# Recurrent state by one scan per head pair, and rows placed by matmul in the first unit

## The chip, the cores and the metric

The kernel runs on one core of one Trainium2 chip. The metric is the device time of one execution in microseconds. TensorE's granted clock has two levels, 1.2 and 2.4 GHz; a granted clock of 1.00 in the profile is the higher one.

## The reference

Three layers follow each other: a recurrent attention with decay over 4 sequences of 768 tokens with 8 heads of 48, a feed-forward layer with g = h cos h, and one with the largest of three products.

```python
def _attn_ref(q, k, v, alpha) -> np.ndarray:
    ...
    for t in range(S):
        state = alpha[:, :, t, :, None] * state + np.einsum('bhd,bhe->bhde', k[:, :, t], v[:, :, t])
        y[:, :, t] = np.einsum('bhd,bhde->bhe', q[:, :, t], state)

def _moe_ref(x, w_in, w_out) -> np.ndarray:
    h = x @ w_in
    g = h * np.cos(h)
    return (g @ w_out).astype(np.float32)

def _moe2_ref(x, w1, w2, w3, w_out) -> np.ndarray:
    h = np.maximum(np.maximum(x @ w1, x @ w2), x @ w3)
    return (h @ w_out).astype(np.float32)
```

There are 3072 tokens, d_model is 384, d_ff is 2048 in the first layer and 768 in the second. All inputs are fp32.

## The kernel before

The tokens are cut into six units of 512 (eight chunks of 64; twelve chunks make a sequence). A unit goes through attention, through 16 tiles of the first layer (one per 128 columns of w_in) and later through the second layer. To keep precision a matrix is split into a high and a low fp32r part, and a product is three matmuls: high by high, high by low, low by high.

**Attention** (`att`) is called for each unit and for four head pairs, pair 3 first, then 0, 1, 2. For a pair the two heads lie on partitions 0 to 47 and 64 to 111. Scans on VectorE build g, the products of decays from a token to the end of its chunk (L370 in the first unit, L380 in the others), and their counterpart in al (L376, L385). GpSimd multiplies k and q by them (L372, L384, L387). TensorE transposes k (L392), makes the scores (L404) and each chunk's own contribution to the state (L409). ScalarE or VectorE and GpSimd mask the scores into the tile a (L416, L417, L420).

The state s at the start of each chunk is then built step by step in `state`: eight instructions on VectorE (L426, L428), each of which takes the one before it, multiplies by the chunk's whole decay g[:, c, 0] and adds the chunk's own contribution out of PSUM. The state that the values need, d, is s times g once more: on GpSimd (L440), two products of 48 x 384 per pair, and in the first unit on ScalarE for the first head, chunk by chunk (L435). TensorE adds scores by v (L453) and d by q (L459) in PSUM. ScalarE takes the high part of the result into the tile xt (L474). The low part is taken by VectorE (L481), or in the first unit by a product with minus the identity (L477) and ScalarE (L479).

A tile of xt has 128 rows for each of the pairs 0, 1 and 2: 2 x 48 of the pair itself, and in the two gaps of 16 rows the rows of pair 3. Pair 3 is therefore made first, into the tile yy, and two DMAs per pair (L488) copy its rows into the gaps. The first layer's products wait for them.

**The first layer** (`moe1`) makes for tile i nine matmuls into a bank of PSUM (L501 to L503: three pieces of x by three products), then cos by a sine of half the argument: L508 and L510, L511 on ScalarE, L509 and L513 or L517 on VectorE, the high part gh on ScalarE and the low part gl on GpSimd (L515, for the tiles below GLP1) or VectorE (L523). Nine matmuls (L528 to L530) add into three banks acc. In the first unit the weights come in while the tiles run: `weight` loads a block (SP queue, L312), unpacks it in three instructions on VectorE (L315 to L317), and splits it on ScalarE (L320) and GpSimd (L321). Each tile has two blocks, one of w_in and one of w_out; 32 blocks in all.

**The order.** Nothing of this runs in the order of the source. Each operation is put into `Program` with a modelled duration, its reads and writes, and a due time; `Program.order` lists them for all engines, and picks on each engine, among the operations that are ready by the model, the one that is due first. The constants at the top (W1E, MOE_EARLY, ATT0, ATTS, GLP1) set due times and choices. On the chip each engine runs its own list in this fixed order.

## Time and profile before

| | |
|---|---|
| median of three runs | 818.61 us (815.3 to 819.21) |
| profiled execution | 816.90 us, its span 815.2 us |
| TensorE, VectorE, ScalarE, GpSimd busy | 791.5, 476.4, 360.9, 192.8 us |
| mean granted clock of TensorE | 0.985 |

A busy matmul row is not TensorE at its peak, because matmuls are pipelined; the distance between the starts of two products tells more. The times in a timeline count from the start of the span. A wait that is put down to an instruction is put down to the one that came last. VectorE's instructions overlap a little: the next one can start before the record of the last one ends.

### The profile page before, as it was taken

To read this page: it belongs to the slowest core of one execution; us is meant where nothing else is said; L and a number is where in the kernel's file an instruction comes from. 1 tells how busy PE (TensorE), PEld (TensorE's weight loads), DVE (VectorE), ACT (ScalarE), POOL (GpSimd) and SP (SyncE) were. 2 spreads that over 40 slices of the span, in tenths; PEclk is the share of its full clock that TensorE was granted. 3 is DMA by queue.
4 is the path that set the end of the run, shared out by engine and by line. 5 is a ranking of instruction groups with operands and counts; after the bars stand their busy time and mean duration, and the time that the engine had idled before them with its cause. 6 is when DMAs were issued, how large, how long until landed. Compare 5 with 4: busy or idle time off the path is not lost.

```text
span 815.2 us, 15114 instructions
## 1 busy us (share of the span) xinstructions
PE 791.5 (97%) x6168; PEld 646.0 (79%) x6168; DVE 476.4 (58%) x924; ACT 360.9 (44%) x667; POOL 192.8 (24%) x191
## 2 busy tenths in 40 slices
PE   7679999999999999999999999999999999999998
PEld 6567778888878878888888788888888888888886
DVE  7988999765786587667679955452232222322221
ACT  4575655555645565555577746531121121112121
POOL 7777876530231023101123200110000000000000
PEclk8789999999999999999999999999999999999999
DMA  9745564430242033103135600412020020200001
GB/s 273 214 132 174 182 209 141 130 93 5 88 147 54 2 115 108 43 1 108 34 107 161 221 23 1 156 58 86 26 83 27 14 91 26 78 27 13 14 27 39
DMA packets 26661, 71.86 MB, mean 88 GB/s; under 512 B 3488, under 2 KB 3488, under 8 KB 26592
## 3 DMA queue, kind: packets, MB, share of 16 engines
q1 hardware_dynamic: 26592, 70.90, 26.9%
q8 instruction: 48, 0.79, 0.4%
q14 instruction: 21, 0.17, 0.1%
HBM read 54.37 MB, written 14.16 MB: 84 GB/s over the span
## 4 chain that ended last, share of the span: by engine, by line
PE 84%; DVE 6%; POOL 4%; issue 2%; DMA 2%; ACT 2%; SPq 0%; POOLq 0%; DVEq 0%; ACTq 0%
PE ps L580 9%; PE ps L579 9%; PE ps L581 9%; PE acc L528 7%; PE ps L501 7%; PE acc L530 7%; PE acc L529 7%; PE ps L503 7%; PE ps L502 7%; PE ps L603 3%; PE ps L602 3%; PE ps L604 3%; PE ps L459 2%; PE ps L404 1%; PE ps L453 1%
## 5 line engine op out<-in xcount | busy, mean ns | idle before, releaser
L501 PE MATMUL ps<-xt,wih 128*128 128x512 f32 x288 | 116.3, 404 | 3.7 <-ACT kt L395 2.2
L528 PE MATMUL acc<-gh,woh 128*128 128x512 f32 x288 | 116.5, 405 | 0.7 <-DVE yy L538 0.5
L530 PE MATMUL acc<-gl,woh 128*128 128x512 f32 x288 | 112.8, 392 | 0.5 <-DVE gl L523 0.4
L502 PE MATMUL ps<-xt,wih 128*128 128x512 f32 x288 | 113.2, 393 | 0.0
L503 PE MATMUL ps<-xt,wil 128*128 128x512 f32 x288 | 113.0, 392 | 0.0
L529 PE MATMUL acc<-gh,wol 128*128 128x512 f32 x288 | 112.4, 390 | 0.0
L517 DVE SCALAR_TENSOR_TENSOR ps<-q,ps 128x512 f32<-128x512 f32 x76 | 52.7, 694 | 56.9 <-ACT q L511 56.7
L589 DVE TENSOR_TENSOR ps<-t,ps 128x512 f32<-128x512 f32 x36 | 25.0, 696 | 103.6 <-PE ps L581 103.5
L510 ACT ACTIVATE q<-q 128x512 f32<-128x512 f32 x96 | 60.5, 631 | 52.3 <-DVE q L509 52.0
L508 ACT ACTIVATE q<-ps 128x512 int32<-128x512 f32 x96 | 57.1, 595 | 57.0 <-PE ps L503 54.6
L509 DVE SCALAR_TENSOR_TENSOR q<-q,ps 128x512 f32<-128x512 int32 x96 | 65.7, 685 | 21.1 <-ACT q L508 20.8
L590 ACT ACTIVATE h<-ps 128x512 fp32r<-128x512 f32 x36 | 21.5, 598 | 112.1 <-DVE ps L589 112.0
L523 DVE TENSOR_TENSOR gl<-ps,gh 128x512 fp32r<-128x512 f32 x76 | 52.1, 686 | 26.7 <-PE ps L503 15.9
L501 PEld LDWEIGHTS ps<-xt,wih 128*128 128x128 f32 x288 | 54.7, 190 | 16.4 <-ACT kt L395 3.2
L440 POOL TENSOR_TENSOR d<-s,g 48x384 f32<-48x384 f32 x44 | 37.0, 842 | 125.5 <-DVE s L428 123.7
L587 DVE TENSOR_TENSOR t<-t,ps 128x512 f32<-128x512 f32 x36 | 24.8, 688 | 71.2 <-PE ps L581 70.4
L528 PEld LDWEIGHTS acc<-gh,woh 128*128 128x128 f32 x288 | 54.0, 188 | 14.9 <-DVE yy L538 2.3
L518 ACT ACTIVATE gh<-ps 128x512 fp32r<-128x512 f32 x76 | 45.4, 598 | 44.0 <-DVE ps L517 41.5
L530 PEld LDWEIGHTS acc<-gl,woh 128*128 128x128 f32 x288 | 54.1, 188 | 13.5 <-DVE gl L523 1.4
L503 PEld LDWEIGHTS ps<-xt,wil 128*128 128x128 f32 x288 | 54.7, 190 | 11.8
L502 PEld LDWEIGHTS ps<-xt,wih 128*128 128x128 f32 x288 | 54.9, 190 | 10.4
L529 PEld LDWEIGHTS acc<-gh,wol 128*128 128x128 f32 x288 | 54.1, 188 | 9.9
(122 smaller groups left out, 1579.4 us busy)
## 6 DMA issues: line engine op xcount, KB each, us to landing
raw<-in_wt SPq DMA_DIRECT2D x56, 384.0 KB, 3.3
kq<-in_qka SPq DMA_DIRECT2D x23, 448.0 KB, 4.2
x1d<-yy SPq DMA_DIRECT2D x18, 512.0 KB, 2.6
xt<-x1d SPq DMA_DIRECT2D x18, 512.0 KB, 4.4
v<-in_vv SPq DMA_DIRECT2D x22, 256.0 KB, 3.2
al<-in_qka SPq DMA_DIRECT2D x24, 228.4 KB, 2.7
outT<-y SPq DMA_DIRECT2D x18, 256.0 KB, 2.0
xt<-yy SPq DMA_DIRECT2D x36, 64.0 KB, 2.6
```

Of the source, the lines that this page charges most:

```text
L501: pe.matmul(ps, wi["h"][:, f, cc], xt[:, cc, 0], start=(cc == 0), stop=False)
L502: pe.matmul(ps, wi["h"][:, f, cc], xt[:, cc, 1], start=False, stop=False)
L503: pe.matmul(ps, wi["l"][:, f, cc], xt[:, cc, 0], start=False, stop=(cc == NR - 1))
L508: op("Act", act(HB, True), lambda: se.activation(q.bitcast(I32), ps, AF.Copy, scale=INV2PI), [hk], [qk], m)
L509: op("DVE", dve(HB), lambda: ve.scalar_tensor_tensor(q, q.bitcast(I32), -TWOPI, ps, ALU.mult, ALU.add), [hk], [qk], m)
L510: op("Act", act(HB), lambda: se.activation(q, q, AF.Sin, scale=0.5), (), [qk], m)
L528: pe.matmul(acc[c], oh, gh, start=(f == 0), stop=False)
L529: pe.matmul(acc[c], ol, gh, start=False, stop=False)
L530: pe.matmul(acc[c], oh, gl, start=False, stop=(f == NF1 - 1))
L579: pe.matmul(ps, w2t["h"][m][:, f, cc], xt[:, cc, 0], start=(cc == 0), stop=False)
L580: pe.matmul(ps, w2t["h"][m][:, f, cc], xt[:, cc, 1], start=False, stop=False)
L581: pe.matmul(ps, w2t["l"][m][:, f, cc], xt[:, cc, 0], start=False, stop=(cc == NR - 1))
```

## The change

1. The state of a pair is made by one scan (L457 of the changed kernel). ScalarE copies the eight own contributions out of PSUM into s, which now has the layout [partition, column e, chunk], ten places per column (two copies, L455; a carry of the last state from the second unit on, L453). GpSimd spreads g[:, c, 0] over the columns into a tile gx (L442), with zeros where a sequence begins (L448). The scan runs over 480 elements: add, then multiply. What it leaves is s times g already, so d is a mere copy with the chunk outermost (L465): by ScalarE in units 0 to 5 as the constants stand.
2. In the first unit the rows of pair 3 are not copied by DMA. A tile sel (in the space of the second gl tile) is built at the start by ScalarE, and four matmuls of 256 columns per pair (L501) add the selected rows of yy into the pair's PSUM before ScalarE takes the high part. In the other units the DMAs stay.
3. There are two g tiles instead of three, one inv instead of two. The constants GLP1 (20 to 24), W1E (10 to 14), MOE_EARLY (4 to 2) and ATTS (2.5 to 3) change, and a coefficient of the modelled matmul time.

```diff
-NQ, NG, NRAW, NIN, NV, NGS = 3, 2, 3, 3, 2, 3
+NQ, NG, NRAW, NIN, NV, NGS = 3, 2, 3, 3, 2, 2
...
-GLP1 = 20
+GLP1 = 24
...
-W1E = 10
-MOE_EARLY = 4
+W1E = 14
+MOE_EARLY = 2
...
-ATTS = 2.5
+ATTS = 3
...
+    sel = gl_b[1][:, 0:(NP - 1) * P].rearrange("p (k n) -> p k n", k=NP - 1)
...
-    s_b = [ap.tile([PR, NC, D], F32, name=f"s{p}") for p in range(NP)]
+    s_b = [ap.tile([PR, D, NC + 2], F32, name=f"s{p}") for p in range(NP)]
+    x_b = [ap.tile([PR, D, NC + 2], F32, name=f"gx{i}") for i in range(1)]
...
-        for c in range(NC - 1):
-            op("DVE", 0.2, lambda c=c: state(c), [rk[c % 2], *kgs, (*sk, c)], [(*sk, c + 1)], t0 + 0.25)
...
-                op("Pool", pool(NC * D), lambda j=j, w=w: ge.tensor_tensor(d[w, j], s[w], g[w, :, 0:1].to_broadcast([D, NC, D]), ALU.mult),
...
+        def spread(e):
+            gc = g.rearrange("p c t -> p t c")[:, 0:1].to_broadcast([PR, D, NC])
...
+                ge.tensor_copy(gx[:, :, 0:NC], gc)
+            for c in range(NC):
+                if firsts[c]:
...
+                        ge.memset(gx[:, :, c:c + 1], 0.0)
...
+        if u:
+            op("Act", 0.25, lambda: se.activation(s[:, :, 0:1], s[:, :, NC:NC + 1], AF.Copy), (), [sk], t0 - 0.5)
+        for h in range(2):
+            op("Act", act(AO, True) + 0.05, lambda h=h: se.activation(
+                s[:, :, 1 + h:NC + 1:2], r[h][0:PR, 0:AO].rearrange("p (i e) -> p e i", e=D), AF.Copy), [rk[h], *([sk] if h else [])], [(sk, h) if h else sk], t0 + 0.22)
+        op("DVE", 0.07 + 0.00208 * D * (NC + 2), lambda: ve.tensor_tensor_scan(
+            s.rearrange("p e c -> p (e c)"), s.rearrange("p e c -> p (e c)"), gx.rearrange("p e c -> p (e c)"), 0.0, ALU.add, ALU.mult),
+           [xk, (sk, 1)], [sk], t0 + 0.25, port=True)
...
+                op("Act", act(NC * D), lambda j=j, w=w, x=x: se.activation(d[w, j], x, AF.Copy), [sk], [(dk, j)], t0 + 0.25)
...
+        moved = u < SELU and p < NP - 1
...
+                        pe.matmul(y[h][:, 0:HB // 2], sel[:, p], yy_b[0][:, x, HB // 2 * h:HB // 2 * (h + 1)], start=False, stop=(x == 1), skip_group_check=True)
...
-        if p < NP - 1:
+        if p < NP - 1 and not moved:
...
+                se.activation(sel[:, p], ident, AF.Copy, scale=0.0)
+                for i in range(2):
+                    row = 16 * (2 * p + i)
+                    src = UP * (row // D) + row % D
+                    se.activation(sel[:, p, UP * i + D:UP * (i + 1)], ident[:, src:src + 16], AF.Copy)
```

The order of the instructions changes on every engine. Buffer numbers in the rows below are the build's own and differ between the two kernels.

TensorE at the end of the first unit's attention, before: acc is where the last pair's values lie, minus gives their low part (L477), and the pieces of x are multiplied by the first weights (L501). The last row is the third piece of tile 0.

```order
L477 MATMUL acc_96<-xt_451,minus 128x256
L501 MATMUL ps_100<-xt_451,wih 128x512
L502 MATMUL ps_100<-xt_451,wih 128x512
L503 MATMUL ps_100<-xt_451,wil 128x512
L501 MATMUL ps_98<-xt_451,wih 128x512
L502 MATMUL ps_98<-xt_451,wih 128x512
L503 MATMUL ps_98<-xt_451,wil 128x512
L392 MATMUL ps_99<-ident,kq_112 128x112 x4
L501 MATMUL ps_99<-xt_451,wih 128x512
L502 MATMUL ps_99<-xt_451,wih 128x512
L503 MATMUL ps_99<-xt_451,wil 128x512
L501 MATMUL ps_100<-xt_451,wih 128x512
```

After: the values with d (L483), the four selecting products (L501), the low part (L510), and the scores of the next unit.

```order
L483 MATMUL acc_95<-yy_91,d_126 48x64 x2
L483 MATMUL acc_96<-yy_91,d_126 48x64 x2
L501 MATMUL acc_95<-yy_90,gl_89 128x256 x2
L501 MATMUL acc_96<-yy_90,gl_89 128x256 x2
L510 MATMUL acc_95<-xt_448,minus 128x256
L510 MATMUL acc_96<-xt_448,minus 128x256
L415 MATMUL ps_100<-kq_110 64x64
L415 MATMUL ps_102<-kq_110 64x64
```

The selecting products stand between the values and the low part, in TensorE's own list; before, TensorE's list went on to products that wait for DMAs.

VectorE in the middle of the second unit's first pair, before: state steps (s_125) between the steps of a weight block and scans.

```order
L315 TENSOR_SCALAR ps_99<-raw_93 128x384
L428 SCALAR_TENSOR_TENSOR s_125<-s_125,g_114,ps_101 112x48
L316 SCALAR_TENSOR_TENSOR ps_99<-raw_93,ps_99 128x384
L428 SCALAR_TENSOR_TENSOR s_125<-s_125,g_114,ps_102 112x48
L317 SCALAR_TENSOR_TENSOR raw_93<-raw_93,ps_99 128x384
L428 SCALAR_TENSOR_TENSOR s_125<-s_125,g_114,ps_101 112x48
L380 SCALAR_TENSOR_TENSOR g_113<-al_107,one_103 112x520
L428 SCALAR_TENSOR_TENSOR s_125<-s_125,g_114,ps_102 112x48
L383 RECIPROCAL inv_104<-g_113 112x8
```

After, at the state of the same pair (s_123): one row stands for the eight.

```order
L326 TENSOR_SCALAR ps_98<-raw_92 128x384
L327 SCALAR_TENSOR_TENSOR ps_98<-raw_92,ps_98 128x384
L546 SCALAR_TENSOR_TENSOR q_84<-q_84,ps_99 128x512
L328 SCALAR_TENSOR_TENSOR raw_92<-raw_92,ps_98 128x384
L457 SCALAR_TENSOR_TENSOR s_123<-s_123,gx_124 112x480
L326 TENSOR_SCALAR ps_102<-raw_93 128x384
L546 SCALAR_TENSOR_TENSOR q_85<-q_85,ps_101 128x512
L327 SCALAR_TENSOR_TENSOR ps_102<-raw_93,ps_102 128x384
L542 SCALAR_TENSOR_TENSOR q_83<-q_83,ps_100 128x512
L328 SCALAR_TENSOR_TENSOR raw_93<-raw_93,ps_102 128x384
```

The scan comes between two weight blocks, and the two-step chain of gelu (L546, L542) goes on around it.

TensorE at tile 13 of the first unit, before: the transposes of a pair (L392), the nine products of tile 13 (L501 to L503, ps_98), behind them the values of another pair (L453).

```order
L503 MATMUL ps_102<-xt_451,wil 128x512
L392 MATMUL ps_98<-ident,kq_110 128x112 x4
L501 MATMUL ps_98<-xt_451,wih 128x512
L502 MATMUL ps_98<-xt_451,wih 128x512
L503 MATMUL ps_98<-xt_451,wil 128x512
L501 MATMUL ps_98<-xt_451,wih 128x512
L502 MATMUL ps_98<-xt_451,wih 128x512
L503 MATMUL ps_98<-xt_451,wil 128x512
L501 MATMUL ps_98<-xt_451,wih 128x512
L502 MATMUL ps_98<-xt_451,wih 128x512
L503 MATMUL ps_98<-xt_451,wil 128x512
L453 MATMUL ps_99<-a_121,v_117 64x64 x2
```

After: the output products (acc) of one more tile come first, then tile 13 (L534 to L536, ps_100).

```order
L561 MATMUL acc_97<-gh_87,woh 128x512
L562 MATMUL acc_97<-gh_87,wol 128x512
L563 MATMUL acc_97<-gl_89,woh 128x512
L534 MATMUL ps_100<-xt_448,wih 128x512
L535 MATMUL ps_100<-xt_448,wih 128x512
L536 MATMUL ps_100<-xt_448,wil 128x512
L534 MATMUL ps_100<-xt_448,wih 128x512
L535 MATMUL ps_100<-xt_448,wih 128x512
L536 MATMUL ps_100<-xt_448,wil 128x512
```

In the list after, the values group that followed tile 13 and one more score group stand before this place too: up to tile 13's first product there are 9 groups of scores, 8 of values and 12 tiles of output products (before: 8, 7 and 11).

## Rows read from the trace of the kernel before

**Rows 1.** The page, busy tenths in 40 slices of 20.4 us, two engines

```profile
PE   7679999999999999999999999999999999999998
...
DVE  7988999765786587667679955452232222322221
```

**Rows 2.** Table of stretches: us, busy of each engine, clock, DMA share, GB/s

```profile
0.00:60.00 60.00, 44.55 (x728) 36.97 (x729) 50.89 (x121) 34.04 (x86) 46.54 (x55) 0.80 0.69 206
60.00:115.00 55.00, 51.51 (x506) 40.60 (x507) 52.19 (x115) 32.11 (x63) 44.44 (x39) 1.00 0.59 182
115.00:450.00 335.00, 335.00 (x3354) 271.64 (x3353) 248.59 (x499) 194.97 (x352) 90.54 (x88) 1.00 0.28 88
...
650.00:700.00 50.00, 50.00 (x222) 41.41 (x221) 13.06 (x19) 8.97 (x15) 0.00 (x0) 1.00 0.12 48
```

**Rows 3.** Timeline of TensorE: start, length, engine, line, operation, tiles, shapes

```profile
78.95 0.49 PE L530 MATMUL acc<-gl,woh 128*128 128x512 f32 x1 [0.15 <-POOL gl L515]
...
81.25 0.39 PE L529 MATMUL acc<-gh,wol 128*128 128x512 f32 x1
...
84.91 0.39 PE L503 MATMUL ps<-xt,wil 128*128 128x512 f32 x1
...
86.63 0.39 PE L529 MATMUL acc<-gh,wol 128*128 128x512 f32 x1
```

**Rows 4.** Timeline, end of the first attention unit (several engines)

```profile
43.46 0.51 SPq L488 DMA_DIRECT2D xt<-yy  x1
...
46.63 0.50 PE L501 MATMUL ps<-xt,wih 128*128 128x512 f32 x1 [0.69 <-ACT kt L395]
...
53.36 0.64 PE L392 MATMUL ps<-ident,kq 112*128 112x112 f32 x4 [3.04 <-DVE raw L317]
...
59.88 0.50 PE L528 MATMUL acc<-gh,woh 128*128 128x512 f32 x1
```

**Rows 5.** Timeline around the weights of tile 13

```profile
107.37 2.42 DVE L385 TENSOR_TENSOR_SCAN al<-al,inv 112x520 f32<-112x520 f32 x1
...
107.67 1.02 POOL L321 TENSOR_TENSOR wol<-raw,woh 128x384 fp32r<-128x384 f32 x1
...
110.95 0.55 DVE L317 SCALAR_TENSOR_TENSOR raw<-raw,ps 128x384 uint32<-128x384 uint32 x1
...
112.56 1.01 POOL L321 TENSOR_TENSOR wil<-raw,wih 128x384 fp32r<-128x384 f32 x1
...
113.88 0.50 PE L501 MATMUL ps<-xt,wih 128*128 128x512 f32 x1 [1.53 <-ACT kt L395]
```

**Rows 6.** Timeline of VectorE, state steps among weight steps and a scan

```profile
43.42 0.55 DVE L315 TENSOR_SCALAR ps<-raw 128x384 uint32<-128x384 uint32 x1
43.88 0.26 DVE L428 SCALAR_TENSOR_TENSOR s<-s,g,ps 112x48 f32<-112x48 f32 x1
44.05 0.55 DVE L316 SCALAR_TENSOR_TENSOR ps<-raw,ps 128x384 uint32<-128x384 uint32 x1
...
45.35 1.23 DVE L380 TENSOR_TENSOR_SCAN g<-al,one 112x520 f32<-112x520 f32 x1
```

**Rows 7.** Groups of instructions by line: busy us, mean ns, idle before them

```profile
L509 DVE SCALAR_TENSOR_TENSOR q<-q,ps 128x512 f32<-128x512 int32 x96 | 65.7, 685 | 21.1 <-ACT q L508 20.8
L440 POOL TENSOR_TENSOR d<-s,g 48x384 f32<-48x384 f32 x44 | 37.0, 842 | 125.5 <-DVE s L428 123.7
L385 DVE TENSOR_TENSOR_SCAN al<-al,inv 112x520 f32<-112x520 f32 x20 | 27.0, 1350 | 0.3
L320 ACT ACTIVATE wih<-raw 128x384 fp32r<-128x384 f32 x16 | 8.9, 559 | 12.5 <-DVE raw L317 11.8 <-DMA v<-in_vv 0.8
...
L638 POOL MEMSET s<- 112x384 f32 x4 | 1.5, 414 | 0.1
```

**Rows 8.** Timeline of the start

```profile
7.83 0.54 ACT L395 ACTIVATE kt<-ps 128x448 f32<-128x448 f32 x1 [5.42 <-PE ps L392]
...
17.40 0.56 DVE L315 TENSOR_SCALAR ps<-raw 128x384 uint32<-128x384 uint32 x1 [0.36 <-DMA raw<-in_wt]
```

73 lines of the change are left out of this document (44 added, 29 removed).

## The prediction

> **What bounds the kernel now.** I read the slices of the page first. The reader is to see that the matmul row is full from the eighth slice to the last but one, while VectorE's row is high in the first eight and falls after that [rows 1]. The table of stretches makes it sharp [rows 2]: from 115 to 450 us TensorE is busy for all 335.00 us at granted clock 1.00, from 60 to 115 us for 51.51 of 55, from 0 to 60 us for 44.55 at a mean clock of 0.80, so partly at the lower of the two levels, 1.2 GHz. Behind 115 us TensorE alone sets the time, and an engine that gets faster there gives nothing. What the change can win must be won in the first 115 us, and must show as matmul work that is done earlier.
>
> For that the pieces of TensorE's work need prices. In the last stage 222 products of 512 columns take 50 us [rows 2], 0.225 us each. A group of 32 score products and 32 state products between two such products moves them from 84.91 to 86.63 us [rows 3]; two steps of 0.225 are their own, so the group costs 1.27 us. A group of values products moves 78.95 to 81.25 in the same way: 1.85 us.
>
> Then the end of the first unit's attention [rows 4]: the last two row copies from yy to xt are issued at 43.46 us, the third piece of the first tile's hidden product starts only at 46.63, TensorE later waits 3.04 us until 53.36, and the first output product (L528) starts at 59.88. From there TensorE is nearly dense.
>
> Last, who paces TensorE between 60 and 115 us. VectorE is busy for 52.19 of these 55 us [rows 2]; it unpacks the weights, three instructions a block. At 110.95 us it comes to the last instruction of the block with tile 13's input weights, GpSimd takes the low part from 112.56, and TensorE, idle for 1.53 us, starts tile 13 at 113.88 [rows 5]. There the weights of VectorE and the work of TensorE meet, and I make the sum at that point.
>
> **The change part by part.**
>
> *State on VectorE.* Between the first weight block and the 27th (the input weights of tile 13), the order has 47 state instructions before; after it has 7 scans of 480 elements instead, one long scan less, two gelu instructions and two half tiles of the x residue more. A state instruction between two others costs 0.17 us from start to start (43.88 to 44.05), 47 of them 8.0 us [rows 6]. But L316 needs the result of L315, which takes 0.55 us; the two start 0.63 apart with a state instruction between them, so that one costs only 0.08, and 47 of them 3.8 us. A scan of 520 elements takes 1.23 us [rows 6], less the 0.09 by which the next instruction overlaps it (0.26 of a state instruction against its 0.17): 1.14; by the same rate 480 elements cost 1.05, seven scans 7.4 us. The missing long scan gives 1.1 back, the two gelu instructions take 2 x 0.6 (group mean 0.685 [rows 7], less the overlap), the two half tiles about half of that each, 0.6. Sum: -8.0 + 7.4 - 1.1 + 1.2 + 0.6 = +0.1 us at the one end, and with 3.8 for 8.0, +4.3 at the other. **VectorE's work is not made smaller**; what is shorter is the chain. VectorE is idle for 2.8 us between 60 and 115 and for 9.1 before [rows 2], so part of a surplus is absorbed. I take +1.0 us for the time at which block 27 is ready, nearer to the lower end for that reason, and keep both ends.
>
> *GpSimd.* It loses the 842 ns products for d [rows 7], one per pair in the first unit and two in the others, and gains one spread of the same 384 elements per pair, which this trace does not show. It lies between a clearing of 384 elements, 0.414 us, and the low part of a weight block of 384 elements, 1.02 us [rows 5]; I take 0.84, the product that also reads g broadcast. At either end GpSimd does less than before from the second unit on. At the start its clearings grow by about 1.0 us (five of 480 elements at 0.414 per 384, 2.6, for four of 384, 1.7, and a strided one), and a spread goes ahead of the first k product: 1.9 us of delay for the first pair. The cover is the wait of the first weight block for its DMA at 17.40 us [rows 8], which stands behind the first pair's work on VectorE; without it the delay would cost its 1.9.
>
> *ScalarE.* Per pair it gets two copies out of PSUM, two copies for d and, from the second unit on, one carry. None has more than 384 columns, for which a copy takes 0.559 us [rows 7]: at most 2.8 us per pair. In the first unit seven short copies for d go, in the others nothing. ScalarE is busy for 195 of 335 us in the long stretch [rows 2], and 16 pairs add at most 45: no cost; without that slack it would be rival 4. The nine instructions that build the selection take at most 9 x 0.56 = 5.0 us, inside the 5.42 us for which ScalarE is idle before 7.83 us [rows 8].
>
> *Selection.* Twelve products of 256 columns at 0.11 us are 1.35 us of new matmul work at full clock. They remove six DMA issues from the SP queue in the first unit, and with them the 3.17 us between issue and third piece (43.46 to 46.63) [rows 4]; in its place stand four products of 0.11 to 0.22. That gives 2.3 to 2.7 us. The chain of this last pair has one scan and two copies for eight dependent steps, but in the new order its scan stands behind three weight blocks, so I add only 0.4: the third piece comes 2.9 us earlier. The values group of the second unit's first pair moves behind the first output product: 1.85 us at full clock, 2.6 at the mixed clock there. So the first output product should start near 59.9 - 2.9 - 2.6 = 54.4 us, of which 1.85 is work put off: a true lead of 3.6 us.
>
> *Order of TensorE.* By the two orders, when tile 13's first product comes TensorE has done, more than before, one score group (1.27), one values group (1.85) and the output products of one more tile (9 x 0.225 = 2.03): **5.15 us of work**. The 1.35 for the selection is new work and counts for nothing. If tile 13 starts 1.0 us later, all that follows comes 5.15 - 1.0 = 4.15 us earlier. TensorE can be there in time: it has 3.6 us of lead and 3.5 us of idle time between 60 and 115 us to use, 7.1 together.
>
> **Sum.** The profiled execution took 816.90 us; the three timed runs have their median at 818.61 and lie from 815.3 to 819.21. 816.9 - 4.15 is 812.75. The mean of the four executions is 817.5, and as the profiled one lies below the median I go by that: **813.3 us**.
>
> **A rule against it.** At 107.37 us a scan takes 2.42 us, while the one at 45.35 takes 1.23 [rows 5, 6]; during the longer one GpSimd works on a weight block from 107.67 for 1.02 us, and the scan ends 1.1 us after that, about its own length. So a scan can be held up by 1.19 us; on the mean of twenty (1.350 us [rows 7]) it is 0.12. The Trainium skill, page "SBUF — State Buffer", section "SBUF: two separate sides", says that a VectorE instruction with two SBUF inputs and a GpSimd instruction that reads SBUF take a shared port by an exclusive lock, and that the loser is blocked for the whole instruction; the 2.42 us agree. By that rule the change adds instructions that can be locked out, since the old state step has an input in PSUM and the scan has both in SBUF, and at its worst the time is that of rival 3.
>
> **Rivals.**
>
> 1. *The lead is larger* (chance 0.15). If block 27 comes 2 us earlier, because VectorE's 2.8 us of idle time go, and TensorE waits nowhere between 60 and 115 us, the gain is the whole 7.1 us: 810.4. For it: the lower end of VectorE's work. Against: its upper end.
>
> 2. *The lead is given back at the weights* (0.27). If VectorE's surplus is the full 4.3 us, tile 13 starts that much later and the gain is 5.15 - 4.3 = 0.85: 816.7. It decides if most state instructions cost 0.08 us. It is also the case in which the state chain was never what TensorE waited for, so that the change does not do what it says. For it: VectorE is busy for 95% of 60 to 115 us.
>
> 3. *Slower, by the lock* (0.08). Seven scans that each meet a GpSimd instruction cost up to 7 x 1.19 = 8.3 us on VectorE before tile 13: 5.15 - 1.0 - 8.3 = -4.2, so 817.5 + 4.2 = 821.7. It decides from 0.6 us of mean hold-up per scan, where the gain is nil. For it: GpSimd is busy for 44.44 of 55 us [rows 2]. Against: the long scans run under the same load with 0.12.
>
> 4. *Slower, by new waits later* (0.05). One buffer for the spread and two for g tie each pair to the one before it. If TensorE waited for 0.5 us per pair in the 16 pairs after the second unit, it would be 8 us: 813.3 + 8 = 821.3. Against: TensorE waits for nothing from 115 to 450 us.
>
> **How the numbers follow.** The forecast has 0.45, from 811 to 816. About 0.5% (4.1 us) is what a measurement of this kernel can tell from no change. Against the median of 818.61, faster means below 814.5: rival 1 and most of the forecast, 0.53. Slower means above 822.7: the worse halves of rivals 3 and 4 and some tail, 0.10. The rest, 0.37, is the upper part of the forecast and rival 2. The range reaches from 806 (rival 1 with a still shorter start) to 820, which leaves out rivals 3 and 4 and the tails, 2 in 10.
>
> **What would show it.** Right: the first output product (L561) between 52 and 56 us; no row copies in the first unit, and the third piece within 2 us of the last copy into x; tile 13 between 112 and 117 us with a short wait before it; no wait of TensorE from 120 to 450 us; scans of 1.1 us. Wrong: L561 no earlier than 58 us (the start was not bound by state and copies); tile 13 after 118 us with VectorE full (rival 2), scans of 1.7 us or more (rival 3), or waits of TensorE for d or acc after 120 us (rival 4).

## The result, and the profile after

The changed kernel takes **822.15 us** (median of 8 runs, 820.15 to 826.0), the kernel before 816.41 (8 runs on the same chip, 815.0 to 819.21). The ratio is 1.0073, with a 95% interval of 1.0055 to 1.0092: 5.7 us slower, by more than the 0.5% that can be told from no change. Forecast was 813.3. The profiled execution of the changed kernel took 825.48 us with a span of 823.8; it is one of the longer ones, so it shows 8.6 us more span than the profile of before, not 5.7.

The page of the changed kernel, the two engines of [rows 1], again in 40 slices:

```profile
PE   6879889999999999999999999999999999999997
...
DVE  7889899955786577656569864563232222322221
```

TensorE has a second dip in its fifth and sixth slice (82 to 124 us), and VectorE is no fuller there than before. The table of stretches, with the columns of [rows 2]:

```profile
0.00:60.00 60.00, 45.19 (x684) 36.79 (x685) 49.59 (x83) 40.02 (x89) 46.27 (x60) 0.83 0.66 197
60.00:115.00 55.00, 50.44 (x604) 39.23 (x604) 49.34 (x83) 37.88 (x76) 38.83 (x35) 1.00 0.58 166
115.00:450.00 335.00, 331.57 (x3278) 266.53 (x3277) 235.16 (x379) 229.81 (x421) 89.06 (x86) 1.00 0.28 84
```

From 60 to 115 us TensorE works 50.44 us instead of 51.51. VectorE, which was to be the pacer, works only 49.34 instead of 52.19, and so leaves 5.66 us idle where it left 2.8. From 115 to 450 us TensorE now idles for 3.43 us; before, not at all. ScalarE has gone from 194.97 to 229.81 us there.

The end of the first unit, which answers to [rows 4]; the columns are start, length, engine, line, operation:

```profile
41.68 0.74 PE L501 MATMUL acc<-yy,gl 128*128 128x256 f32 x4
...
43.80 0.66 ACT L512 ACTIVATE xt<-acc 128x256 fp32r<-128x256 f32 x2 [0.20 <-PE acc L510]
...
45.30 0.59 PE L534 MATMUL ps<-xt,wih 128*128 128x512 f32 x1
...
53.99 0.98 PE L403 MATMUL ps<-ident,kq 112*128 112x112 f32 x4 [2.95 <-POOL wil L332]
...
58.63 0.63 PE L561 MATMUL acc<-gh,woh 128*128 128x512 f32 x1
```

The selecting products (L501) follow at once, and the product that needs the moved rows starts at 45.30 us instead of 46.63, 1.3 us earlier where 2.9 were forecast. But TensorE then waits 2.95 us until 53.99, as it waited 3.04 until 53.36 before, and the first output product (L561) starts at 58.63 us, not at 54.4: the lead is 1.25 us, and 1.85 of work had been put off, so there is none.

The weights of tile 13, which answer to [rows 5]:

```profile
99.79 2.52 POOL L548 TENSOR_TENSOR gl<-q,gh 128x512 fp32r<-128x512 f32 x2
...
99.88 3.53 DVE L391 TENSOR_TENSOR_SCAN g<-al,one 112x520 f32<-112x520 f32 x1
...
119.11 0.56 DVE L328 SCALAR_TENSOR_TENSOR raw<-raw,ps 128x384 uint32<-128x384 uint32 x1
...
120.33 1.03 POOL L332 TENSOR_TENSOR wil<-raw,wih 128x384 fp32r<-128x384 f32 x1
...
122.13 0.39 PE L534 MATMUL ps<-xt,wih 128*128 128x512 f32 x1
```

VectorE ends that block at 119.11 us instead of 110.95, **8.2 us later** where the prediction took 1.0, and tile 13 starts at 122.13 instead of 113.88. But TensorE does not wait for these weights: their low part is done at 121.36 us (120.33 + 1.03), and the product at 122.13 follows the one before it without a gap. Nor did they end the wait of 1.53 us before tile 13 in the kernel before. The row in [rows 5] names kt (L395), ScalarE's copy out of the PSUM bank that tile 13's products go into; it ran until 113.83 us, and the low part of the weights was done at 113.57:

```profile
113.30 0.53 ACT L395 ACTIVATE kt<-ps 128x448 f32<-128x448 f32 x1
```

VectorE's lateness has other signs. A scan of 520 elements takes 3.53 us on the way: it starts 0.09 us after two low parts of the gelu on GpSimd and ends 1.1 us behind their end (99.79 + 2.52 = 102.31, the scan 103.41).

ScalarE's list shows the second thing on the way:

```profile
58.14 1.88 ACT L465 ACTIVATE d<-s 48x384 f32<-48x384 f32 x2
...
58.55 0.68 DVE L542 SCALAR_TENSOR_TENSOR q<-q,ps 128x512 f32<-128x512 int32 x1
...
61.48 0.61 ACT L543 ACTIVATE q<-q 128x512 f32<-128x512 f32 x1
...
62.45 0.61 ACT L544 ACTIVATE q<-q 128x512 f32<-128x512 f32 x1
...
63.09 0.69 DVE L546 SCALAR_TENSOR_TENSOR q<-q,ps 128x512 f32<-128x512 f32 x1 [2.20 <-ACT q L544]
```

VectorE's first step of a tile's gelu is done at 59.23 us (58.55 + 0.68), and the sine of it (L543) is ScalarE's. But there two copies for d started at 58.14 (1.88 us for the two, in the row's count), a carry and the rounding of another tile (L547, which itself waited 0.59 us for TensorE) stand ahead; the sine starts at 61.48, a split of weights follows, the square starts at 62.45, and VectorE, which needs it for L546, has waited for 2.20 us at 63.09. Such a wait is new: from 60 to 115 us VectorE waits 2.2 us for the square and 1.9 for loads of weights; before, it waited 1.8 for loads and never for the square.

The groups by line that matter, with busy us, mean ns and idle time before them, as in [rows 7]:

```profile
L465 ACT ACTIVATE d<-s 48x384 f32<-48x384 f32 x48 | 44.5, 926 | 10.1 <-DVE s L457 9.3
...
L457 DVE TENSOR_TENSOR_SCAN s<-s,gx 112x480 f32<-112x480 f32 x24 | 29.1, 1212 | 3.4 <-ACT s L455 3.4
...
L391 DVE TENSOR_TENSOR_SCAN g<-al,one 112x520 f32<-112x520 f32 x20 | 28.5, 1435 | 3.4 <-POOL gx L442 3.4
...
L396 DVE TENSOR_TENSOR_SCAN al<-al,inv 112x520 f32<-112x520 f32 x20 | 27.8, 1388 | 0.2
...
L442 POOL COPY gx<-g 112x384 f32<-112x384 f32 x24 | 21.2, 884 | 123.9 <-DVE s L457 123.8
...
L455 ACT ACTIVATE s<-ps 112x192 f32<-112x192 f32 x48 | 17.7, 384 | 10.1 <-PE ps L420 7.9 <-DVE a L431 2.1
```

The copies for d (L465) take 926 ns, not 559. The state scans (L457) take 1.21 us on the mean, where 1.05 was worked out; the gate scans L391 rose from 1.251 us (24.9 us for the same twenty) to 1.435; the spread (L442) takes 0.88, where 0.84 was taken. What TensorE waits for, in total us, times, longest:

```profile
PE acc L483 <- ACT d L465: 3.5, 4, 1.3
...
PE ps L403 <- POOL wil L332: 3.0, 1, 3.0
...
PE ps L536 <- POOL wil L332: 2.1, 3, 1.2
...
PE ps L483 <- ACT d L465: 1.1, 2, 0.6
```

The first and the last line are new: 4.6 us of waits for d. Of these 3.5 us lie before 58 us, in the first unit, 0.6 between 58 and 125 us and 0.5 behind that. The third line is new too: in the kernel before no hidden product waits for its weights, here four of them do between 96 and 117 us (these 2.1 us, and 1.4 for a high part on ScalarE).

### The profile page after: what moved, and what is told of

It is laid out like the page before. It is cut to its first block, busy times and chain, and to the rows that moved or that the text cites. A ratio compares the mean times of both kernels' runs of the same rounds, so it can differ in the third digit from the quotient of the medians.

```text
span 823.8 us, 15046 instructions
## 1 busy us (share of the span) xinstructions
PE 795.2 (97%) x6180; PEld 645.7 (78%) x6180; DVE 468.1 (57%) x751; ACT 413.7 (50%) x764; POOL 189.1 (23%) x193
## 4 chain that ended last, share of the span: by engine, by line
PE 77%; issue 5%; DVE 4%; ACT 4%; POOL 4%; DMA 4%; SPq 1%; POOLq 0%; DVEq 0%; ACTq 0%
PE ps L613 9%; PE ps L614 9%; PE ps L612 9%; PE acc L561 7%; PE acc L563 6%; PE acc L562 6%; PE ps L534 6%; PE ps L536 6%; PE ps L535 6%; PE ps L636 3%; PE ps L637 3%; PE ps L635 3%; DMA raw<-in_wt 3%; PE ps L483 1%; PE ps L415 1%
## 5 line engine op out<-in xcount | busy, mean ns | idle before, releaser
L534 PE MATMUL ps<-xt,wih 128*128 128x512 f32 x288 | 117.1, 407 | 3.5 <-DVE raw L328 2.0
L561 PE MATMUL acc<-gh,woh 128*128 128x512 f32 x288 | 116.8, 405 | 1.3 <-DVE yy L571 0.9
L536 PE MATMUL ps<-xt,wil 128*128 128x512 f32 x288 | 114.7, 398 | 2.1 <-POOL wil L332 2.1
L563 PE MATMUL acc<-gl,woh 128*128 128x512 f32 x288 | 113.2, 393 | 1.2 <-POOL gl L548 0.9
L542 DVE SCALAR_TENSOR_TENSOR q<-q,ps 128x512 f32<-128x512 int32 x96 | 65.6, 683 | 26.9 <-ACT q L541 26.0
L543 ACT ACTIVATE q<-q 128x512 f32<-128x512 f32 x96 | 60.6, 631 | 40.2 <-DVE q L542 39.9
L550 DVE SCALAR_TENSOR_TENSOR ps<-q,ps 128x512 f32<-128x512 f32 x72 | 49.7, 690 | 50.2 <-ACT q L544 50.1
L534 PEld LDWEIGHTS ps<-xt,wih 128*128 128x128 f32 x288 | 55.4, 192 | 15.9 <-DVE raw L328 2.6
L556 DVE TENSOR_TENSOR gl<-ps,gh 128x512 fp32r<-128x512 f32 x72 | 49.4, 687 | 31.8 <-ACT gh L551 18.6
L536 PEld LDWEIGHTS ps<-xt,wil 128*128 128x128 f32 x288 | 55.4, 192 | 15.4 <-POOL wil L332 3.7
L563 PEld LDWEIGHTS acc<-gl,woh 128*128 128x128 f32 x288 | 54.1, 188 | 16.0 <-DVE gl L556 2.3
L561 PEld LDWEIGHTS acc<-gh,woh 128*128 128x128 f32 x288 | 54.2, 188 | 15.5 <-DVE yy L571 2.8
L551 ACT ACTIVATE gh<-ps 128x512 fp32r<-128x512 f32 x72 | 43.1, 598 | 41.6 <-DVE ps L550 40.0
L544 ACT ACTIVATE q<-q 128x512 f32<-128x512 f32 x96 | 60.2, 627 | 1.7
```

Source lines behind the costliest of these rows:

```text
L534: pe.matmul(ps, wi["h"][:, f, cc], xt[:, cc, 0], start=(cc == 0), stop=False)
L536: pe.matmul(ps, wi["l"][:, f, cc], xt[:, cc, 0], start=False, stop=(cc == NR - 1))
L542: op("DVE", dve(HB), lambda: ve.scalar_tensor_tensor(q, q.bitcast(I32), -TWOPI, ps, ALU.mult, ALU.add), [hk], [qk], m)
L543: op("Act", act(HB), lambda: se.activation(q, q, AF.Sin, scale=0.5), (), [qk], m)
L544: op("Act", act(HB), lambda: se.activation(q, q, AF.Square), (), [qk], m)
L561: pe.matmul(acc[c], oh, gh, start=(f == 0), stop=False)
```

## The experiments

Two things have to be said first. The planner walks through a set of names where it opens an instruction's banks, and Python draws the order of such a set anew in each process: two builds of one file differ in the banks and in the order of some neighbours on the engines. All kernels below have this fixed. And the kernel before was run beside each group: its medians were 817.33 (a_fixed, a_flat_d, a_d_transposed, a_short_pool), 817.86 (b_sel, b_const, a_old_const, a_no_sel), 817.55 (b_sel_const, a_write_turned, a_pool_share, a_priced) and 818.04 (a_flat_short, a_no_d, b_no_state). Ratios are to those; each group ran on another chip, so a difference between two groups is given by the ratios as well. Theory 1: the copies for d hold up ScalarE's list. Theory 2: GpSimd holds up VectorE's scans. Theory 3: the order that the new constants give is worse. Theory 4: VectorE gains nothing from losing the state steps.

**a_fixed**, the base.

```diff
-            for k in {*reads, *writes}:
+            for k in dict.fromkeys([*reads, *writes]):
```

> The changed kernel with one edit in the planner: the banks of an instruction are walked in the order in which they are listed, not in that of a set of names, which Python draws anew for every build. So each build has the same order of instructions; it is the base for the runs that keep this order. If the loss lies in the work itself (theory 1 or 2 below), the time stays within 820 to 824 us, as the changed kernel's 822.15. If it is the luck of one order (theory 3), it can lie up to 5 us off, and its own runs should spread less than the 820.15 to 826.0 of the changed kernel.

Measured: 824.01 us (820.86 to 824.85), ratio 1.0069 [1.0044, 1.0093]. The loss is there in the base too. That does not settle theory 3: in the traces a_fixed has, line by line, the same order on every engine as the profiled execution of the changed kernel, so it is no second order (a_priced below is one). Its runs spread by 4.0 us, those of the changed kernel by 5.9; later kernels with one fixed order spread by up to 7.5 (b_no_state), so such a spread needs no second order.

**a_flat_d**, the copies for d read neighbours.

```diff
-            x = s[w, :, 0:NC].rearrange("p e c -> p c e")
+            x = s[w].rearrange("p e c -> p (e c)")[:, 0:NC * D].rearrange("p (c e) -> p c e", c=NC)
```

> In the order of a_fixed, the two ScalarE copies per pair that make d read 384 neighbouring elements instead of a strided view (the states then stand at wrong places in d; nothing else changes). Theory 1: the copies of 926 ns hold up ScalarE's list, and behind it the weight splits and the gelu. Flat ones should take about 0.56 us, 48 x 0.37 = 17.8 us less on ScalarE, tile 13 should start 2 us earlier or more, TensorE's waits for d (4.6 us in the changed kernel) should fall below 2, and the time by 3 to 5 us against a_fixed. Theory 2 (VectorE's scans held up by GpSimd) and theory 3 (the order): within 1 us of a_fixed.

Measured: **819.24 us**, ratio 1.0012 [0.9992, 1.0031], 4.8 us below a_fixed. The group of the copies in this kernel:

```profile
L465 ACT ACTIVATE d<-s 48x384 f32<-48x384 f32 x48 | 25.1, 522 | 10.7 <-DVE s L457 9.7 <-DVE acc L386 0.4
```

The copies fell to 0.522 us and TensorE's waits for d from 5.6 us to 2.3. Theory 1 stands: 4.8 us of the loss is the length of these copies. Two marks were missed: the waits for d did not fall below 2 us, and tile 13 starts at 120.88 us, not earlier than a_fixed's 120.28. This execution came to the first output product 2.56 us later (59.26 against 56.70; up to 60 us its granted clock is 0.83, a_fixed's 0.86), so that from there to tile 13 it took 61.62 us instead of 63.58. From tile 13 to the end it took 698.22 us instead of 702.52, with the same 4812 matmuls at a granted clock of 1.00 in both: 4.3 us, more than half of the gain behind the first output product, is won where the prediction had no cost. Of these 4.3 us, 1.9 are idle time of TensorE, and 2.4 are matmul records that are longer in a_fixed. One place in a_fixed:

```profile
306.92 0.58 ACT L570 ACTIVATE yy<-acc 128x512 fp32r<-128x512 f32 x1
...
308.38 0.50 PE L561 MATMUL acc<-gh,woh 128*128 128x512 f32 x1 [0.46 <-DVE yy L571]
```

and in a_flat_d:

```profile
305.69 0.58 ACT L570 ACTIVATE yy<-acc 128x512 fp32r<-128x512 f32 x1
...
307.39 0.40 PE L561 MATMUL acc<-gh,woh 128*128 128x512 f32 x1
```

ScalarE takes a finished unit out of the banks acc (L570), VectorE adds its part (L571), and TensorE's next output product needs the bank. With the long copies ahead in its list ScalarE comes to it 1.23 us later (0.37 of that is a_flat_d's lead up to there), TensorE waits 0.46 us and the product behind the wait takes 0.50 us for 0.40; a_flat_d's lead grows from 0.37 to 1.10 us within these few products.

**a_d_transposed**, the copies run along rows and TensorE reads the stride.

```diff
-    d_b = [ap.tile([PR, 2, NC, D], F32, ...
+    d_b = [ap.tile([PR, 2, D, NC], F32, ...
-   ... d[:, j, c], qv3[:, c] ...
+   ... d[:, j, :, c], qv3[:, c] ...
-            x = s[w, :, 0:NC].rearrange("p e c -> p c e")
+            x = s[w, :, 0:NC]
```

> In the order of a_fixed, d is kept in the layout of the state (48 x 8 instead of 8 x 48), so that the copies run along their rows, and the matmuls of the values group read their weights with a stride of 8 elements. The whole computation is done. Theory 1: as a_flat_d, if TensorE reads such weights at the same price (28 products per pair; their group of 0.98 us in the changed kernel shows it): 3 to 5 us below a_fixed. If the strided weights cost TensorE as much as ScalarE saves, 24 pairs lose up to 24 x 1 us: up to 20 us slower. Theories 2 and 3: no gain.

Measured: 828.26 us, ratio 1.0112 [1.0077, 1.0146]. ScalarE's copies took 0.524 us, but the weight loads of the values group rose. The group of these loads and one values group with the product behind it, in a_fixed:

```profile
L483 PEld LDWEIGHTS ps<-kq,d 112*48 112x48 f32 x592 | 18.0, 123 | 2.9 <-ACT d L465 1.6
...
208.06 0.99 PE L483 MATMUL ps<-kq,d 112*48 112x64 f32 x28
...
208.98 0.50 PE L561 MATMUL acc<-gh,woh 128*128 128x512 f32 x1
```

and in a_d_transposed:

```profile
L483 PEld LDWEIGHTS ps<-kq,d 112*48 112x48 f32 x592 | 29.1, 188 | 1.4
...
209.70 1.50 PE L483 MATMUL ps<-kq,d 112*48 112x64 f32 x28
...
211.14 0.50 PE L561 MATMUL acc<-gh,woh 128*128 128x512 f32 x1
```

A load takes 188 ns instead of 123, and the 28 products 1.44 us instead of 0.92 from start to the next product. 24 pairs at 0.52 are 12.5 us, of which part falls into TensorE's idle time (25.4 us in a_flat_d, 19.8 here, span less busy time); 9.0 us more than a_flat_d were measured. TensorE pays more than ScalarE saves.

**a_write_turned** (run later, it belongs here), turned on the side of the writes.

```diff
-            x = s[w, :, 0:NC].rearrange("p e c -> p c e")
+            x = s[w, :, 0:NC]
-  ... se.activation(d[w, j], x, AF.Copy)
+  ... se.activation(d[w, j].rearrange("p c e -> p e c"), x, AF.Copy)
```

> In the order of a_fixed, the copies for d read the state along its rows and turn it on the side of the writes instead of the reads; the whole computation is done. If ScalarE's price is that of a strided read, they take about 0.52 us as the flat ones, and the time is that of a_flat_d, 818 to 820.5. If it is the price of turning, on either side, they take about 0.92 us and the time is that of a_fixed, 823 to 825.

Measured: 821.9 us, ratio 1.0062 [1.0038, 1.0086], and for the copies:

```profile
L465 ACT ACTIVATE d<-s 48x384 f32<-48x384 f32 x48 | 43.3, 903 | 10.1 <-DVE s L457 9.4
```

0.903 us: turning costs on either side. The median lies 2.1 us below a_fixed's and outside both expected ranges; by the ratios it is 0.6 us, within the noise. The Trainium skill, page "SBUF — State Buffer", section "Door 1: The DMA port swizzle (why `[64,N]` ≈ `[32,N]`)", has a note that SBUF has lines of 16 bytes, and that each access that goes on to another line pays a penalty. The runs agree on that: steps of 40 bytes (read) and 192 bytes (written) cost 0.40 and 0.38 us per 384 elements over the flat copy. That note spoke against this change and the prediction did not use it.

**a_short_pool**, GpSimd's low parts of the gelu cut short.

```diff
- ge.tensor_tensor(gl, q, gh.bitcast(F32), ALU.subtract)
+ ge.tensor_tensor(gl[:, 0:8], q[:, 0:8], gh.bitcast(F32)[:, 0:8], ALU.subtract)
```

> In the order of a_fixed, GpSimd's low parts of the gelu (1.28 us each for 512 columns, 24 tiles) are cut to 8 of 512 columns, so the low part of g is left out in the rest, and five short copies on ScalarE at the start fill its buffers. Theory 2: scans of VectorE that meet a GpSimd instruction wait for it (3.53 us at 99.88 in the changed kernel while two of these low parts ran, where a free one takes 1.24). Without them the scans behind 50 us should all take 1.15 to 1.3 us, tile 13 come 2 to 3 us earlier and the time fall by 2 to 4 us. Theory 1: at most 1 us. Theory 3: less than 1 us.

Measured: 821.82 us, ratio 1.0036 [1.0014, 1.0058], 2.2 us below a_fixed. The place of the longest scan, in a_fixed:

```profile
97.95 2.52 POOL L548 TENSOR_TENSOR gl<-q,gh 128x512 fp32r<-128x512 f32 x2
...
98.09 3.48 DVE L391 TENSOR_TENSOR_SCAN g<-al,one 112x520 f32<-112x520 f32 x1
```

and here:

```profile
97.65 0.20 POOL L548 TENSOR_TENSOR gl<-q,gh 128x8 fp32r<-128x8 f32 x1
...
97.75 1.23 DVE L391 TENSOR_TENSOR_SCAN g<-al,one 112x520 f32<-112x520 f32 x1
...
98.19 0.79 POOL L548 TENSOR_TENSOR gl<-q,gh 128x8 fp32r<-128x8 f32 x1 [0.34 <-ACT gh L547]
```

In a_fixed the scan waits for both low parts (97.95 + 2.52 = 100.47) and ends 1.1 us after them; here it takes 1.23. Tile 13's weights are ready on VectorE at 114.66 us instead of 117.25, and that difference is the gate scans' alone, as the table further down shows. So 2 us of the loss go with GpSimd's low parts, as theory 2 has it, but perhaps not by the scans alone: the edit also empties GpSimd's own list, and TensorE's waits for GpSimd's weights and low parts (L403 and L536 for wil, L563 for gl) fell from 5.9 us in a_fixed to 2.9. No run parts the two. Not all scans came free: one of 2.01 us is left at 105.59, beside a weight block.

**b_sel**, the kernel before with the selection alone (the code of the change under `moved` and `setup_sel`, nothing else).

> The kernel before, with the selection alone: in the first unit the last pair's rows are added by twelve selecting products instead of six row copies; the state, its copies and all planner constants stay as before (and the order is the same in each build). By the prediction's term the selection gives 2.3 to 2.7 us at the end of the first unit and costs nothing but its 1.35 us of matmul work: if that lead reaches the end, 1 to 2.5 us faster than before; if the first gelu and the weights set the pace there, as in the changed kernel, where the first output product came at 58.63 instead of 59.88, within 1 us of before or up to 1.35 slower. Theory 1 (the copies for d) and theory 3 (the planner's constants): no loss here.

Measured: 820.44 us, ratio 1.0048 [1.0024, 1.0071], slower, which was not expected. The first output product comes at 55.24 us, near the forecast 54.4 (here too the values group of the second unit's first pair has moved behind it, to 61.7). The lead is then given back. The profiled execution took 824.06 us, longer than the median. Two of TensorE's waits (L510 is the hidden product, L539 the output product):

```profile
PE ps L510 <- DVE q L522: 3.0, 2, 1.8
...
PE acc L539 <- POOL gl L524: 2.3, 2, 1.8
```

Both are waits for the gelu, 5.3 us together, where the kernel before has 0.6 for its low part and none for its VectorE step. Of them 1.3 us lie before the first output product, the rest between 120 and 143 us. It looks as if with the old due times TensorE came to the gelu before it is ready; no run tests that. Two longer waits, 2.7 us at 24.68 and 3.8 us at 51.94, the profile puts down to nothing.

**b_const**, the kernel before with the new constants alone (GLP1 24, W1E 14, MOE_EARLY 2, ATTS 3, 0.25 for 0.375).

> The kernel before, with the changed kernel's planner constants alone (GLP1 24, W1E 14, MOE_EARLY 2, ATTS 3, a matmul's fixed cost 0.25). Theory 3 (the constants put the work in a worse order): 2 to 5 us slower than before, with tile 13 later. Theory 1: the loss comes from the copies for d, so within 1.5 us of before.

Measured: 817.49 us, ratio 0.9995 [0.9981, 1.0009]. Theory 3 falls.

**a_old_const**, the changed kernel with the old constants.

> The changed kernel with the planner constants of the kernel before (GLP1 20, W1E 10, MOE_EARLY 4, ATTS 2.5, fixed cost 0.375), states and selection as in the change. Theory 3: 3 us or more faster than a_fixed (824.0), near the kernel before. Theory 1: the copies for d stay, so within 2 us of a_fixed or slower.

Measured: 832.18 us, ratio 1.0172 [1.0152, 1.0193], 8.2 us slower than a_fixed (8.4 by the ratios): theory 3 falls from this side too. The new constants are worth nothing to the kernel before and much to the changed one.

**a_no_sel**, the changed kernel with SELU = 0.

> The changed kernel without the selection: the six row copies by DMA of the first unit are back, the states by scan stay. By the prediction's term the first output product comes 2.3 to 2.7 us later than in a_fixed and the time is 1 to 2.5 us longer (825 to 826.5). If the selection gives nothing, as theory 1 reads the first unit, the time is that of a_fixed less the 1.35 us of selecting products: 822.5 to 824.

Measured: 828.75 us, ratio 1.0136 [1.0115, 1.0158], 4.7 us slower than a_fixed (5.5 by the ratios), and the first output product starts at 64.00 us instead of 56.70. Beside the scans the selection is worth more than was forecast; alone with old constants it cost 2.6. The parts do not add.

**b_sel_const**, the change without its states by scan.

> The kernel before with the selection and the changed kernel's constants, so the change without its states by scan. Against a_fixed (824.0) it prices the states alone. Theory 1 (the copies for d are what costs): 818 to 820, a_fixed less the 4.8 us that the flat copies gave, or below. Theory 4 (VectorE gains nothing: the state steps lay in gaps between the weight instructions, and the long scans are held up by GpSimd): 814 to 818, at or below before, with the block of tile 13's weights on VectorE at 110 to 112 us instead of 117 to 119. If the selection is at fault whatever stands around it (b_sel was 2.6 us slower), 820 to 823.

Measured: **816.72 us**, ratio 0.9986 [0.9974, 0.9998]. It is 0.1% below the kernel before, less than the 0.5% that can be told from no change, so level with it. The loss of the change is in the states: a_fixed less b_sel_const is 7.3 us (6.8 by the ratios). Tile 13's weights come to their last VectorE step at 113.15 us, 1.2 us later than theory 4 had it and 2.2 later than before, and yet the time is that of the kernel before.

**a_pool_share**, GpSimd copies d for one head.

```diff
-DCA = (1, 2, 3, 4, 5)
-DC0 = "AA"
+DCA = ()
+DC0 = "AP"
```

> The changed kernel in which GpSimd makes the copy for d of one head of each pair and ScalarE that of the other (the planner orders it anew). ScalarE loses 22 us of copies; GpSimd gains 24 of 0.85 to 0.95 us. Theory 1: faster than a_fixed by 2 to 4 us if GpSimd has room. Theory 2 (scans held up by GpSimd): six or seven more GpSimd instructions before tile 13 hold up scans for up to 1 us each, so no gain or 1 to 4 us slower.

Measured: 825.18 us, ratio 1.0078 [1.0055, 1.0101]: no gain. GpSimd's copies take 0.998 us, and TensorE waits 6.3 us in five waits for the k and q products of GpSimd (3.8 and 2.5).

**a_priced**, the planner knows the price.

```diff
- op("Act", act(NC * D), ...
+ op("Act", 0.9, ...
```

> The changed kernel with the planner's duration of a copy for d set to 0.90 us (it has 0.42; they take 0.92), so that the planner can put other work around them. Theory 1 with a planner misled by the price: 2 to 5 us faster than a_fixed, waits of TensorE for d below 2.5 us. If the copies' length itself is the cost, or the order is settled by due times: within 1.5 us of a_fixed.

Measured: 822.87 us, ratio 1.0055 [1.0034, 1.0075], 1.1 below a_fixed, which is not clear of noise. TensorE's waits for d fell to 1.4 us as expected, but others came: 4.2 us for a weight block of GpSimd's and 7.0 for its k and q products. The order is another one on every engine, and the loss is there. A planner that knew the price would not have saved the change.

**a_flat_short**, both edits of a_flat_d and a_short_pool.

> In the order of a_fixed, both edits at once: flat copies for d (wrong states in d) and GpSimd's gelu low parts cut to 8 columns (low part left out). If the length of the copies (4.8 us) and the hold-up of the scans (2.2 us) are the whole price of the states (7.3 us, a_fixed against b_sel_const), the time is 816 to 818, level with b_sel_const's 816.72. If the two cover each other, 819 or more; if a third cost is left, also 819 or more.

Measured: **815.94 us**, ratio 0.998 [0.9962, 0.9998]. The two costs add (8.1 us below a_fixed, 7.3 by the ratios, for 4.8 and 2.2): without them the scans are level with b_sel_const, and no better. They are as large as the whole loss. That they are the whole loss of the states is not shown to the end, since b_sel_const makes the same 24 low parts on GpSimd in full, and no run cuts them there.

**a_no_d**, no copies for d at all.

```diff
- lambda j=j, w=w, x=x: se.activation(d[w, j], x, AF.Copy)
+ lambda: None
```

> In the order of a_fixed, without any of the 48 copies for d (d stays zero, so the products of q with the state add nothing; the matmuls still run). ScalarE loses all 44 us of them. If ScalarE's length goes on paying at the rate of a_flat_d (4.8 us for 17.8 of copies), 811 to 814, and the scans would win if their result had the layout that TensorE wants. If only the part over the old price counted, because the chain and VectorE bind then, 817 to 819.5.

Measured: 819.13 us, ratio 1.002 [1.0001, 1.004], the same as a_flat_d. ScalarE gives nothing below the flat price: what the prediction had written off as hidden is hidden at 0.52 us a copy, and not at 0.92.

**b_no_state**, b_sel_const without VectorE's 192 state instructions.

```diff
-            if firsts[c]:
-                ve.tensor_copy(o, kvc)
-            else:
-                ve.scalar_tensor_tensor(o, s[:, c], g[:, c, 0:1], kvc, ALU.mult, ALU.add)
+            pass
```

> The order of b_sel_const with all 192 state instructions of VectorE left out (the states stay zero; the products for d and all else run): the bound on what taking work from VectorE's state steps can give. By the prediction's own price at the upper end (0.17 us each, 62 of them before tile 13's weights take 12 us) and its rule that tile 13 follows VectorE, tile 13's weights come 8 us earlier or more and the time falls by 6 us or more, to 810 or below. Theory 4 (half of the steps lie in gaps between the weight instructions, which open again without them, and TensorE waits for other things as well): the weights come 3 to 7 us earlier and the time falls by 1 to 4 us, to 813 to 816.

Measured: 815.69 us, ratio 0.9976 [0.9954, 0.9998], 1.0 us below b_sel_const (0.8 by the ratios), which the intervals do not tell from nothing. Tile 13's weights come 1.2 us earlier (111.94 against 113.15), less than either theory said; the time is in theory 4's range. The stretch from 60 to 115 us in b_sel_const, with the columns of [rows 2]:

```profile
60.00:115.00 55.00, 49.84 (x545) 39.30 (x544) 52.56 (x113) 32.00 (x62) 44.00 (x39) 0.97 0.63 187
```

and without the state instructions:

```profile
60.00:115.00 55.00, 51.45 (x558) 40.29 (x558) 51.14 (x91) 33.95 (x65) 45.12 (x40) 1.00 0.67 193
```

22 instructions fewer on VectorE, and 1.42 us less of its time.

## Why the prediction was wrong

The forecast was 4.15 us gained at tile 13 and nothing behind it. The two profiles in the prediction's own terms, from the first output product to tile 13 and from there to the end, with the columns of [rows 2]; before:

```profile
59.88:113.88 54.00, 50.51 (x505) 39.78 (x501) 51.23 (x113) 31.11 (x61) 43.90 (x39) 1.00 0.60 184
113.88:815.20 701.32, 696.54 (x4940) 569.39 (x4940) 374.42 (x692) 295.81 (x522) 102.43 (x99) 1.00 0.21 71
```

and after:

```profile
58.63:122.13 63.50, 57.87 (x691) 44.59 (x690) 57.67 (x102) 44.21 (x86) 47.33 (x42) 1.00 0.60 173
122.13:823.80 701.67, 693.53 (x4812) 565.45 (x4810) 362.17 (x571) 330.77 (x591) 96.88 (x94) 1.00 0.22 70
```

Tile 13 starts 8.25 us later. TensorE has then done the 5.15 us more of work that the two orders promised, so by the prediction's prices 3.1 us are lost at this point. From there to the end it needs 701.67 us instead of 701.32, though 5.15 us less of work were left: another 5.5 us are lost. Together that is the 8.6 us between the two profiles.

**The path failed.** The prediction let tile 13 follow VectorE's block 27. It did not: tile 13 starts without a wait, 0.77 us after the low part of its weights, and before the change it was kt that came last. The sum at tile 13 is TensorE's own. The first output product comes 1.25 us earlier, 7.4 us more of matmul time stand between it and tile 13 (7.0 by the prediction's prices: 5.15 and the values group of 1.85 that moved), and 2.1 us more of waiting (5.6 for 3.5; of the 5.6 us 3.5 are for weights of earlier tiles, so late weights do reach TensorE, but there). So the 3.6 us of lead were not there, and the 3.5 us of idle time were not used but grew. And "Behind 115 us TensorE alone sets the time" was read off the kernel before and does not carry over: TensorE idles for 8.1 us behind tile 13, before for 4.8.

**The step on ScalarE failed**: "None has more than 384 columns, for which a copy takes 0.559 us" and "no cost". The row was of a flat copy and these turn their elements: 0.926. And slack as a share of a long stretch (195 of 335 us) says nothing of what stands behind a copy in the engine's own list. This step is 4.8 of the 7.3 us. What it holds up is seen in a_fixed against a_flat_d: 4.3 us of the gain lie behind tile 13, one part of it where ScalarE empties the banks acc.

**The step on VectorE failed** too: "I take +1.0 us for the time at which block 27 is ready". It was +8.2 in the profiled execution and +6.3 in a_fixed's, above the upper end of +4.3. The table sorts VectorE's time up to the last instruction of tile 13's weight block, each instruction from its start to the next start, less the idle time before that; us, from the timelines.

```
                       before  after  a_fixed  a_flat_d  a_short_pool  b_sel_const  b_no_state
block ready at         110.95  119.11  117.25   117.88     114.66        113.15       111.94
weights (81)             39.9    42.9    42.7     42.7       42.8          40.6         43.7
state                    12.0     9.9     9.5     10.4        9.7          12.3          -
gate scans (27 to 29)    26.6    29.1    29.1     29.1       26.5          28.8         32.5
gelu (22, then 24)       13.3    14.7    14.7     14.6       14.6          14.4         14.9
idle                      9.1    12.3    10.9     10.8       10.8           6.2          9.9
```

By terms, before to after: the state itself gave 2.1 back, and the weight instructions took 3.0 of it again, since the steps had lain in gaps that the three dependent instructions of a block leave. Over the prediction's own stretch, from the first weight block on, the 47 steps took 8.7 us and the weight instructions rose by 2.9: a step cost 0.12 us, between the 0.17 and the 0.08 of the two ends (b_no_state against b_sel_const gives 0.12 too: 9.1 us of steps, 3.1 back). The seven scans took 8.7 us as well, where 7.4 were worked out. The gelu came out as forecast (1.4 for 1.2). The gate scans cost 2.5 more for one scan fewer, by hold-ups; the prediction had only spoken of the state scans there, and these were held up less (1.21 us). Idle time grew by 3.2 us, but 2.6 of that lie before the first weight block, which starts at 17.66 us, before at 17.40, and cost next to nothing, as the prediction's cover has it. From 60 to 115 us VectorE is idle for 2.85 us more, 2.2 of them in the wait for the square that is shown above; the prediction had let idle time there absorb a part instead.

**The lead at the end of the first unit**: the term for the selection is not what failed (b_sel: 55.24 us for 54.4; a_no_sel against a_fixed: 64.00 and 56.70). In the changed kernel the first output product comes at 58.63 in the profiled execution, 56.70 in a_fixed's: in this unit TensorE waits 3.5 us for d, which the prediction put at nothing. The 2.6 us "at the mixed clock" of the values group has no row; at the clock of 0.80 in [rows 2] it would be 2.3.

**"VectorE's work is not made smaller; what is shorter is the chain"** was right, and should have been the forecast: then nothing is left to gain but the 5.15 us of TensorE's order, which only count if tile 13 comes no later. b_no_state shows how little VectorE's time alone gives: 12.3 us of steps are taken out, and block 27 comes 1.2 us earlier, since 3.1 us come back in the weight instructions, 3.7 in gate scans that are held up and 3.7 in waiting for others.

**The rivals.** Rival 2 (the lead given back at the weights) and rival 3 (the lock) came together in part, with 3.0 us in the weight instructions and 2.5 in the gate scans. The prediction priced each alone, at 816.7 and 821.7, and gave their sum no chance. Rival 3's rule met another victim: the hold-ups hit the old scans, since GpSimd's low parts stand elsewhere in the new order. Its row was read too simply. The scan at 107.37 us started while GpSimd was still at another product, until 107.70, and the weight block at 107.67 was queued behind that:

```profile
106.51 1.19 POOL L384 TENSOR_TENSOR kq<-kq,g 112x512 f32<-112x512 f32 x1 [0.39 <-DMA kq<-in_qka]
```

So this scan waited for two, as the one at 99.88 us does after. Rival 4 (waits for d later on) is hardly there: only 0.5 of the 4.6 us lie behind 125 us. GpSimd's spread (0.88 for 0.84) was priced right, the state scan (1.15 to 1.21 for 1.05) nearly.

What stays open: which waits make up all of the 5.5 us behind tile 13, beyond those for d and for the banks acc; how the 2 us of a_short_pool part between VectorE's scans and GpSimd's own list; how much of b_sel's loss is the due times and how much the order's own accident, as no run changed one of the constants alone; and whether the hold-ups could be had out by an order, since a_short_pool took the work away instead.

## What to carry to other kernels

Price a copy by a row of the same access pattern, not of the same count: here a copy that turns its elements took 1.8 times as long as a flat one, on whichever side it was turned. Work that is put on an engine with slack is still in that engine's list, and what stands behind it there (here the sine of the gelu and the emptying of the banks acc) is what to look at. Before replacing small steps, see what their removal alone would give: here 12.3 us of them, taken out of VectorE's list, brought a weight block 1.2 us forward. And read in the row itself what ended a wait before putting it down to the engine that looks fullest.

## What the runs showed that was not expected

- ScalarE: 384 elements on 48 partitions take 0.522 us along rows, 0.922 read with a step of 40 bytes, 0.903 written with a step of 192 bytes.
- TensorE: a weight load of 48 columns takes 188 ns from elements 32 bytes apart, 123 from neighbours; the group of 28 products goes from 0.92 to 1.44 us.
- VectorE: a scan that starts just after a GpSimd instruction with another one queued behind it waited for both here (3.48 us for 1.23; in the kernel before 2.42, at 107.37 us). The long hold-up came at the same place in the order in a_fixed, a_flat_d, a_d_transposed and a_write_turned, 3.48 to 3.53 us each.
